# Softmax inverses from a logarithm, an exponential and one Newton step, a first pair of heads in three units, and a new order of the attention's work

## The chip, the cores and the metric

The kernel runs on one core of one Trainium2 chip. A core has five engines that run side by side, each with its own instruction stream that it works through in order: TensorE (PE, matrix products; its weight loads are listed as PEld), VectorE (DVE), ScalarE (ACT), GpSimd (POOL) and SyncE (SP, which here only issues DMA transfers). They wait for one another through semaphores. The metric is the device time of one execution in microseconds. An engine that waits for a semaphore holds up everything that stands behind it in its own stream, so the order in which work is written to the streams decides as much as the amount of it.

## The reference

```python
def _attn_ref(q, k, v):                     # 2 x 8 heads, 1152 rows, 64 wide
    q_pool = q.reshape(B, H, S // 2, 2, D).mean(axis=3)      # 576 pooled queries
    scores = scale * np.matmul(q_pool, k.transpose(0, 1, 3, 2))
    scores = scores - np.max(scores, axis=-1, keepdims=True)
    attn = np.exp(scores)
    attn = attn / (np.sum(attn, axis=-1, keepdims=True) + 1e-09)
    return np.matmul(attn, v)

def _moe_ref(x, w_in, w_out):               # 1152 x 512, 2048 hidden
    h = x @ w_in
    g = np.maximum(h, 0.0) + np.log1p(np.exp(-np.abs(h)))
    return g @ w_out

def _moe2_ref(x, w1, w2, w3, w_out):        # 768 hidden
    h = np.maximum(np.maximum(x @ w1, x @ w2), x @ w3)
    return h @ w_out
```

All of it is float32, and the weights arrive as 64-bit floats. The attention's output goes through the first dense block, and that one's through the second.

## The kernel before

**Two stages.** First the attention of 16 heads, taken as 8 pairs; then the dense blocks, which are one long chain of products on PE. The kernel computes a fast form of the attention with ordinary f32r products and checks at the end, with one flag, that its sums were in a safe range; a slower exact form stands behind a branch (`guarded`) and is not run here. Only the fast form (the `else` branch) and the flag are touched by the change.

**A pair of heads, first pass.** `add_q` adds neighbouring queries, `turn_q` and `turn_k` transpose on PE, `high_q`, `low_q`, `high_k`, `low_k` split them into a high and a low part, and `send_q`, `send_q3`, `send_k`, `send_k3` move these by DMA into the stacked operands `q1`, `q3`, `k1`, `k3`. `scores` then multiplies 9 rows of queries (128 each) with the keys in three groups of 384, each into one bank, and `part_max` on DVE reduces each bank to a maximum (tile `nh`, 27 reductions a pair). `whole_max` joins the three groups (`nm`), `turn_m` transposes the maxima on PE, `keep_m` copies them on ACT, and `send_m` puts them by DMA into the last row of `q3`, from which the second pass subtracts them inside the product. This happens in two steps: six rows, then three.

**A pair of heads, second pass: two units.** A unit is one half of a pair's queries: 288 columns for both heads. For each of 9 key blocks j, `turned` computes the transposed scores of both heads (tile `st`, two products each), `exps` exponentiates them on ACT into one of 9 buffers (`p`), `add_p` adds the block to a running sum `acc` over 2 x 288 columns (7 of a unit's 8 adds on POOL, the last on DVE), and `values` multiplies with v into the bank `x` (in two groups, after 4 and after 9 blocks). Then `sum_up` (tile `l`) sums `acc` over the partitions on PE, `keep_sum` copies it on ACT into `rr` and adds the 1e-9, `inverse` takes the reciprocal on DVE in one instruction, `divide` multiplies it with `x` into the output `xy`, and `note` adds the inverses into `low_sums` on POOL for the flag. A unit has one of two `x` banks; all other products share six single banks. After the second unit of pairs 0 to 3, `high_x` and `low_x` split the output for the dense stage.

**Weights.** Nine of the dense blocks' weight tiles are made during the attention: `load_weight` (SP), `size_weight` (ACT), `bound_weight` (POOL, tile `size`), three steps of `float_weight` (DVE, tile `t`), `high_weight` (ACT), `low_weight` (DVE, tile `wl`). Their place is behind everything else (`late`), so they go wherever the planner sees an engine free.

**What sets the order.** `Order` is a planner that runs when the kernel is built. Each piece of work is added with an engine, an assumed duration and a place (a due time); the planner starts, at each engine that comes free, the piece with the lowest place that could start then, and the result is written into the streams. The assumed durations are therefore part of the program: before the change a step of `float_weight` is taken to last 0.5 to 0.7, `low_weight` 0.69, `inverse` 0.45, an add on DVE 0.8, an add on POOL 1.4.

```python
                    engine = "DVE" if j in ON_DVE else "POOL"        # ON_DVE = (8,)
                    order.add(engine, 1.4 if engine == "POOL" else 0.8, p, add_p, u, j, engine,
            order.add("DVE", 0.45, p - 3, inverse, u, writes=(f"rr{u % 2}",))
            order.add("POOL", 0.85, p, note, u, reads=(f"rr{u % 2}",), writes=("low",))
                    order.add("DVE", (0.5, 0.7, 0.7)[step], late + 2 + step, float_weight, n, step,
```

## Time and profile before

| | us |
|---|---|
| median of three runs | 663.94 (663.5 to 664.76) |
| the profiled execution: its own time | 661.27 |
| the profiled execution: span of its trace | 659.5 |
| first product of the second pass (tile `st`) | 31.15 |
| first product of the dense stage | 293.54 |

| share of the span | PE | DVE | ACT | POOL |
|---|---|---|---|---|
| busy | 93% | 69% | 48% | 62% |

The profile is one execution, 1.77 us longer outside the trace than inside. The attention fills the first 293.5 us of it and the dense stage the other 366.0 us; the dense stage keeps PE busy 97% of the time, the attention does not. The busy shares are averages over both, so the attention is read stretch by stretch: which engine has no idle time left in a stretch, and how long a unit takes there. The granted clock (PEclk) is the share of full speed that PE was allowed; PE has two levels, 2.4 and 1.2 GHz.

### The profile page before, as it was taken

The numbers are of one execution on the slowest core, as the hardware profiler recorded it, in microseconds if no ns is written. First come the engines' busy times: TensorE is split into PE (matmuls) and PEld (weight loads), VectorE is DVE, ScalarE is ACT, GpSimd is POOL, SyncE is SP. The second block draws the span as 40 slices with busy tenths as digits, with TensorE's granted clock in tenths as the row PEclk, the third lists the DMA queues.
The fourth block names the chain that finished last, engine by engine and source line by source line (L and its number), as shares of the span: only waits on it lengthen the run. The fifth ranks groups of instructions, "written<-read, shape, count | busy, mean of one in ns | idle before, by whom it ended". The sixth has DMA issues, their size and how long they took to land.

```text
span 659.5 us, 10134 instructions
## 1 busy us (share of the span) xinstructions
PE 610.3 (93%) x3548; PEld 531.5 (81%) x3548; DVE 455.6 (69%) x769; ACT 319.7 (48%) x769; POOL 406.4 (62%) x338
## 2 busy tenths in 40 slices
PE   4899999689886999977999999999999999999995
PEld 3677777457564677656999999999999999999995
DVE  4957777997899887449888888898888852222221
ACT  3245556345453565546677767776664321111111
POOL 6179898867886698877988878789794500000000
PEclk9899999799788999998999999999999999999998
DMA  7997697557626470002333433332233400000001
GB/s 175 199 201 186 125 236 177 150 136 171 157 59 169 104 185 10 1 1 65 99 95 111 127 100 114 95 125 94 67 90 104 126 1 30 20 0 18 32 1 53
DMA packets 60621, 66.14 MB, mean 100 GB/s; under 512 B 22224, under 2 KB 48912, under 8 KB 60560
## 3 DMA queue, kind: packets, MB, share of 16 engines
q1 hardware_dynamic: 59712, 64.62, 37.3%
q10 hardware_dynamic: 848, 0.77, 0.5%
q8 instruction: 30, 0.49, 0.3%
q14 instruction: 31, 0.25, 0.1%
HBM read 43.52 MB, written 2.36 MB: 70 GB/s over the span
## 4 chain that ended last, share of the span: by engine, by line
PE 78%; DVE 12%; POOL 4%; issue 2%; DMA 1%; ACT 1%; SPq 0%; POOLq 0%; ACTq 0%; DVEq 0%
PE bank_h_m L1260 17%; PE bank_h L1260 15%; PE bank_y L1260 15%; PE x L1033 8%; PE bank_o L1260 6%; PE st L1008 5%; PE s L958 4%; PE st L1009 4%; DVE nh L964 3%; DVE rr L1054 2%; POOL acc L1025 2%; DVE t L255 1%; PE tk L914 1%; DVE t L246 1%; POOL size L235 1%
## 5 line engine op out<-in xcount | busy, mean ns | idle before, releaser
L1025 POOL TENSOR_TENSOR acc<-acc,p 128x576 f32<-128x576 f32 x96 | 139.3, 1451 | 19.2 <-ACT p L1018 13.4
L1018 ACT ACTIVATE p<-st 128x288 f32<-128x288 f32 x288 | 101.2, 411 | 75.0 <-PE st L1009 67.7
L964 DVE TENSOR_REDUCE nh<-s 128x1 f32<-128x384 f32 x216 | 106.7, 548 | 33.6 <-PE s L958 30.6
L1260 PE MATMUL bank_h_m<-x,wh 128*128 128x384 f32 x432 | 113.2, 336 | 0.0
L1260 PE MATMUL bank_h<-x,wh 128*128 128x384 f32 x384 | 106.4, 340 | 0.4 <-DVE gl L1337 0.4
L235 POOL TENSOR_SCALAR size<-size 128x512 f32<-128x512 f32 x56 | 85.4, 1528 | 17.2 <-ACT size L230 17.0
L1008 PE MATMUL st<-q,k 128*128 128x288 f32 x288 | 88.3, 321 | 5.4 <-DVE nh L964 5.3
L1009 PE MATMUL st<-q,k 65*128 65x288 f32 x288 | 82.6, 301 | 0.0
L1033 PE MATMUL x<-p,v 128*64 128x288 f32 x576 | 81.5, 430 | 0.0
L1260 PEld LDWEIGHTS bank_h_m<-x,wh 128*128 128x128 f32 x432 | 78.3, 188 | 0.7
L1260 PE MATMUL bank_h_m<-x,wl 128*128 128x384 f32 x216 | 72.5, 335 | 0.0
L1260 PEld LDWEIGHTS bank_h<-x,wh 128*128 128x128 f32 x384 | 71.1, 191 | 1.2 <-DVE gl L1337 0.7
L1008 PEld LDWEIGHTS st<-q,k 128*128 128x128 f32 x288 | 56.0, 195 | 18.9 <-DVE nh L964 7.8
L958 PE MATMUL s<-k,q 128*128 128x384 f32 x192 | 63.3, 385 | 6.9 <-ACT p L1018 3.9
L1260 PE MATMUL bank_y<-gh,wh 128*128 128x384 f32 x192 | 65.4, 341 | 4.0 <-ACT gh L1332 2.3
L1313 POOL TENSOR_TENSOR d<-e,d 128x384 f32<-128x384 f32 x48 | 49.1, 1023 | 27.5 <-DVE d L1306 25.4
L1033 PEld LDWEIGHTS x<-p,v 128*64 128x64 f32 x576 | 40.5, 144 | 31.5 <-issue 10.8
L1260 PE MATMUL bank_h<-x,wl 128*128 128x384 f32 x192 | 65.3, 340 | 0.0
L1260 PE MATMUL bank_y<-gl,wh 128*128 128x384 f32 x192 | 65.2, 340 | 0.0
L1260 PE MATMUL bank_y<-gh,wl 128*128 128x384 f32 x192 | 65.0, 339 | 0.0
L1009 PEld LDWEIGHTS st<-q,k 65*128 65x128 f32 x288 | 56.0, 194 | 0.0
L958 PEld LDWEIGHTS s<-k,q 128*128 128x128 f32 x192 | 35.2, 201 | 20.6 <-DVE nh L964 7.0
(228 smaller groups left out, 1126.7 us busy)
## 6 DMA issues: line engine op xcount, KB each, us to landing
raw<-in_moe_w_out_dram SPq DMA_DIRECT2D x22, 512.0 KB
raw<-in_moe_w_dram SPq DMA_DIRECT2D x18, 512.0 KB
raw<-in_moe_w_in_dram SPq DMA_DIRECT2D x16, 512.0 KB
k<-kh SPq DMA_DIRECT2D x28, 288.0 KB
k<-in_k_dram SPq DMA_DIRECT2D x16, 288.0 KB
v<-in_v_dram SPq DMA_DIRECT2D x16, 288.0 KB
k<-kl SPq DMA_DIRECT2D x15, 288.0 KB
q<-qh SPq DMA_DIRECT2D x29, 144.0 KB
```

The lines of the kernel that those rows point to most:

```text
L235: nc.gpsimd.tensor_scalar(out=size, in0=size, scalar1=SMALLEST, scalar2=None, op0=ALU.max)
L246: nc.vector.tensor_scalar(out=t, in0=size, scalar1=3, scalar2=REST, op0=ALU.logical_shift_left, op1=ALU.bitwise_and,)
L958: nc.tensor.matmul(to, q1[:, i, c0 : c0 + QB], k1[:, i, cols], start=True, stop=True)
L964: nc.vector.tensor_reduce(out=tiles["nh", pr][:, at, g : g + 1], in_=tiles[n][:, :BK], axis=AX.X, op=ALU.max, negate=True)
L1008: nc.tensor.matmul(to, k1[:, i, cols], q_of(pr, i, b * HQ, (b + 1) * HQ), start=True, stop=False)
L1009: nc.tensor.matmul(to, k3[:, i, cols], q3[:, i, b * HQ : (b + 1) * HQ], start=False, stop=True)
L1018: nc.scalar.activation(out=tiles["p", u, j][:, some[0]], in_=tiles[n][:, :HQ], func=AF.Exp)
L1025: engine.tensor_tensor(out=acc, in0=tiles["p", u, 0] if j == 1 else acc, in1=tiles["p", u, j], op=ALU.add)
L1033: nc.tensor.matmul(x[halves(i)], tiles["v", u // 2][:, i, j], tiles["p", u, j][:, i], start=(j == 0), stop=(j == NJ - 1),)
L1054: nc.vector.reciprocal(tiles["rr", u], tiles["rr", u])
L1260: nc.tensor.matmul(ps, lhs(a, kk), rhs(bb, kk), start=start and n == 0, stop=stop and n == last)
L1313: nc.gpsimd.tensor_tensor(out=d, in0=gs["e", i], in1=d, op=ALU.subtract)
```

## The change

**Inverse.** The reciprocal on DVE goes. ACT takes the logarithm of the sum (`log_sum`) and the exponential of its negative (`near_inverse`), and DVE improves that by one Newton step in two instructions (`inverse`, steps 0 and 1); `divide` takes the sign back. The flag's second sum now comes out of the exponential, and `note` and `low_sums` go.

**Adds.** POOL makes all 8 adds of every unit but the last; in the last unit DVE makes all 8.

**Units.** The first pair's queries are cut in three units (128, 224, 224 columns), which makes 17 units in all. Its maxima are taken in another order of rows and in three steps, and its shift rows are written by products with the identity whose single output row ACT copies into `q3` (`row_m`, `keep_row`), without a DMA. `values` works in three groups of three blocks.

**Order.** The assumed durations are set to others, and all places (`AK`, `WINDOW`) change.

```diff
-ON_DVE = (8,)
-VALUES = ((0, 1, 2, 3), (4, 5, 6, 7, 8))
+ON_DVE = ((), ())
+VALUES = ((0, 1, 2), (3, 4, 5), (6, 7, 8))
+XB = 2
+LAST = (1, 2, 3, 4, 5, 6, 7, 8)
...
+        UNIT = [(0, 0, P), (0, P, (NQ - P) // 2), (0, (NQ + P) // 2, (NQ - P) // 2)]
+        UNIT += [(pr, b * HQ, HQ) for pr in range(1, NPAIR) for b in range(2)]
+        FIRST_ROWS = (0, 5, 4, 1, 6, 2, 7, 3, 8)
+        FIRST_STEPS = ((0, 3), (3, 7), (7, 9))
...
+        def row_m(step, n):
+            a, z = rows_of(0, step)
+            tm = bank(n, f"tm_0_{step}")
+            for k, x in enumerate(sorted(FIRST_ROWS[a:z])):
+                at = FIRST_ROWS.index(x)
+                nc.tensor.matmul(tm[D : D + 1, k * P : (k + 1) * P], maxima(0)[:, at : at + 1], ident, start=True, stop=True)
+
+        def keep_row(step, part, n):
+            a, z = rows_of(0, step)
+            k, r, count = runs(sorted(FIRST_ROWS[a:z]))[part]
+            nc.scalar.copy(shift_row(0)[:, r * P : (r + count) * P], tiles[n][D : D + 1, k * P : (k + count) * P])
...
-        def inverse(u):
-            nc.vector.reciprocal(tiles["rr", u], tiles["rr", u])
-        def note(u):
...
+        def log_sum(u):
+            tiles["rz", u] = sm.tile([P, HQ], F32, tag="rz", name=f"rz_{u}")
+            W = UNIT[u][2]
+            nc.scalar.activation(out=tiles["rz", u][:, :W], in_=tiles["rr", u][:, :W], func=AF.Ln)
+
+        def near_inverse(u):
+            rz = tiles["rz", u][:, : UNIT[u][2]]
+            nc.scalar.activation(out=rz, in_=rz, func=AF.Exp, scale=-1.0, accum_out=sums[:, 1, u : u + 1])
+
+        def inverse(u, step):
+            W = UNIT[u][2]
+            rr, rz = tiles["rr", u][:, :W], tiles["rz", u][:, :W]
+            if step == 0:
+                nc.vector.tensor_tensor(out=rr, in0=rr, in1=rz, op=ALU.mult)
             else:
+                nc.vector.scalar_tensor_tensor(out=rr, in0=rr, scalar=2.0, in1=rz, op0=ALU.subtract, op1=ALU.mult)
...
-                    engine = "DVE" if j in ON_DVE else "POOL"
-                    order.add(engine, 1.4 if engine == "POOL" else 0.8, p, add_p, u, j, engine,
+                    engine = "DVE" if j in (ON_DVE[u % 2] if u + 1 < UNITS else LAST) else "POOL"
+                    order.add(engine, 1.5 * part if engine == "POOL" else 1.25 * part, p, add_p, u, j, engine,
...
-                    order.add("DVE", (0.5, 0.7, 0.7)[step], late + 2 + step, float_weight, n, step,
+                    order.add("DVE", (1.2, 1.25, 1.25)[step], late + 2 + step, float_weight, n, step,
```

The dense stage's code and its order on every engine are the same before and after. Three places in the streams show what moved. In the names the first number is the unit (in `nh`, `nm` and `s` the pair), the second the key block or query row, and the last one is only the tile's running number.

POOL, one unit in the stretch where weights are made. Before, unit 6 (from its first add to the next `low_sums`):

```order
L1025 TENSOR_TENSOR acc_6_1601<-p_6_0_1555,p_6_1_1589 128x576
L235 TENSOR_SCALAR size_2_1612<-size_2_1612 128x512
L1025 TENSOR_TENSOR acc_6_1601<-acc_6_1601,p_6_2_1596 128x576
L1025 TENSOR_TENSOR acc_6_1601<-acc_6_1601,p_6_3_1631 128x576
L1025 TENSOR_TENSOR acc_6_1601<-acc_6_1601,p_6_4_1656 128x576
L812 TENSOR_TENSOR qs_6_1705<-q_6_1342 128x2x4x64
L817 TENSOR_TENSOR qt_6_1707<-qm_6_1343 64x128
L1025 TENSOR_TENSOR acc_6_1601<-acc_6_1601,p_6_5_1695 128x576
L1025 TENSOR_TENSOR acc_6_1601<-acc_6_1601,p_6_6_1718 128x576
L1025 TENSOR_TENSOR acc_6_1601<-acc_6_1601,p_6_7_1732 128x576
L1060 TENSOR_TENSOR low_sums_121<-low_sums_121,rr_5_1792 128x288
```

and after, unit 6 again:

```order
L1061 TENSOR_TENSOR acc_6_1534<-p_6_0_1482,p_6_1_1496 128x576
L1061 TENSOR_TENSOR acc_6_1534<-acc_6_1534,p_6_2_1526 128x576
L1061 TENSOR_TENSOR acc_6_1534<-acc_6_1534,p_6_3_1552 128x576
L1061 TENSOR_TENSOR acc_6_1534<-acc_6_1534,p_6_4_1564 128x576
L237 TENSOR_SCALAR size_0_1468<-size_0_1468 128x512
L1061 TENSOR_TENSOR acc_6_1534<-acc_6_1534,p_6_5_1617 128x576
L237 TENSOR_SCALAR size_1_1498<-size_1_1498 128x512
L1061 TENSOR_TENSOR acc_6_1534<-acc_6_1534,p_6_6_1652 128x576
L1061 TENSOR_TENSOR acc_6_1534<-acc_6_1534,p_6_7_1672 128x576
L1061 TENSOR_TENSOR acc_6_1534<-acc_6_1534,p_6_8_1684 128x576
```

POOL now makes the eighth add and no `low_sums`; the sizes of the first weights, which stood in units 5 and 6, come a unit later (in all, one or two a unit until unit 15).

DVE, the end of a unit where weights begin. Before, around the inverse of unit 4:

```order
L974 TENSOR_REDUCE nm_3_1_1550<-nh_3_1193 128x3
L246 TENSOR_SCALAR t_0_1553<-size_0_1380 128x512
L255 SCALAR_TENSOR_TENSOR t_0_1553<-raw_0_1252,t_0_1553 128x512
L259 SCALAR_TENSOR_TENSOR t_0_1553<-raw_0_1252,t_0_1553 128x512
L1054 RECIPROCAL rr_4_1566<-rr_4_1566 128x288
L1066 TENSOR_TENSOR xy_99<-x_4_1240,rr_4_1566 128x288
L246 TENSOR_SCALAR t_1_1594<-size_1_1474 128x512
L1025 TENSOR_TENSOR acc_5_1390<-acc_5_1390,p_5_8_1538 128x576
L255 SCALAR_TENSOR_TENSOR t_1_1594<-raw_1_1383,t_1_1594 128x512
```

and after, around the inverse of unit 5:

```order
L977 TENSOR_REDUCE nh_3_1346<-s_3_7_2_1632 128x1
L1103 TENSOR_TENSOR rr_5_1634<-rr_5_1634,rz_5_1646 128x288
L1105 SCALAR_TENSOR_TENSOR rr_5_1634<-rr_5_1634,rz_5_1646 128x288
L1117 SCALAR_TENSOR_TENSOR xy_99<-x_5_1348,rr_5_1634 128x288
L977 TENSOR_REDUCE nh_3_1346<-s_3_8_0_1667 128x1
L977 TENSOR_REDUCE nh_3_1346<-s_3_8_1_1670 128x1
L977 TENSOR_REDUCE nh_3_1346<-s_3_8_2_1674 128x1
L994 TENSOR_REDUCE nm_3_1567<-nh_3_1346 128x3
L248 TENSOR_SCALAR t_0_1711<-size_0_1468 128x512
```

The inverse now stands in front of the last reductions and no weight stands in front of it; the nine weights are spread over units 6 to 15, about one a unit, where they stood in units 4 to 10.

PE, where the second pass begins. Before:

```order
L958 MATMUL s_0_8_2_323<-k1_0_181,q1_0_102 128x384
L914 MATMUL tk_1_0_328<-ident_94,k_1_284 128x128 x3
L914 MATMUL tk_1_1_333<-ident_94,k_1_284 128x128 x3
L914 MATMUL tk_1_2_344<-ident_94,k_1_284 128x128 x3
L841 MATMUL tq_2_0_350<-ident_94,qs_2_272 128x128 x3
L841 MATMUL tq_2_1_356<-ident_94,qs_2_272 128x128
L845 MATMUL tq_2_1_356<-ident_94,qt_2_274 128x64
L980 MATMUL tm_0_1_365<-ident_94,nm_0_1_362 3x128
L1008 MATMUL st_0_0_0_371<-q1_0_102,k1_0_181 128x288
```

and after:

```order
L966 MATMUL s_0_3_2_337<-k1_0_154,q1_0_102 128x384
L1030 MATMUL tm_0_0_345<-ident_94,nm_0_275 1x128 x3
L966 MATMUL s_0_8_0_350<-k1_0_154,q1_0_102 128x384
L966 MATMUL s_0_8_1_354<-k1_0_154,q1_0_102 128x384
L966 MATMUL s_0_8_2_358<-k1_0_154,q1_0_102 128x384
L1044 MATMUL st_0_0_0_360<-q1_0_102,k1_0_154 128x128
L1045 MATMUL st_0_0_0_360<-q3_0_111,k3_0_112 128x128
```

The first product of the second pass no longer stands behind the last maxima of the pair and pair 2's query transposes; it needs the maxima of three rows and their copy, and the last two rows' maxima are taken while it runs.

## Rows read from the trace of the kernel before

**Rows 1.** Busy time by stage: start:end, length, PE, PEld, DVE, ACT, POOL, PEclk, DMA share, GB/s
```profile
31.10:93.80 62.70, 62.41 (x422) 47.21 (x423) 45.40 (x85) 35.58 (x106) 50.19 (x39) 1.00 0.80 181
93.80:231.20 137.40, 114.89 (x696) 83.20 (x698) 119.78 (x175) 66.72 (x183) 105.90 (x75) 0.89 0.58 144
231.20:271.70 40.50, 40.50 (x282) 30.51 (x281) 29.97 (x52) 24.19 (x72) 34.24 (x25) 1.00 0.31 80
...
293.50:659.50 366.00, 354.72 (x1966) 345.28 (x1964) 231.01 (x406) 174.83 (x363) 184.60 (x162) 0.99 0.23 71
```

**Rows 2.** Chain of waits in time: start, length; first values of units 0, 4, 11, 14, 15
```profile
35.58 2.09 PE x L1033 x16
...
93.78 2.09 PE x L1033 x16
...
231.21 2.09 PE x L1033 x16
...
271.74 2.09 PE x L1033 x16
...
282.44 2.09 PE x L1033 x16
```

**Rows 3.** Groups of POOL instructions, 98 to 210 us: xcount, busy us, mean ns, idle before
```profile
L1025 POOL TENSOR_TENSOR acc<-acc,p 128x576 f32<-128x576 f32 x35 | 52.7, 1506 | 5.0 <-ACT p L1018 3.3
L235 POOL TENSOR_SCALAR size<-size 128x512 f32<-128x512 f32 x8 | 13.3, 1660 | 0.0
L1025 POOL TENSOR_TENSOR acc<-p,p 128x576 f32<-128x576 f32 x6 | 10.6, 1767 | 0.0
L1060 POOL TENSOR_TENSOR low_sums<-low_sums,rr 128x288 f32<-128x288 f32 x6 | 4.8, 800 | 17.0 <-DVE rr L1054 17.0
L288 POOL TENSOR_TENSOR x<-xy,x 128x384 fp32r<-128x384 f32 x3 | 3.9, 1292 | 0.0
...
L817 POOL TENSOR_TENSOR qt<-qm 64x128 f32<-64x128 f32 x3 | 2.0, 660 | 0.0
```

**Rows 4.** Groups of POOL instructions, 30 to 98 us
```profile
L1025 POOL TENSOR_TENSOR acc<-acc,p 128x576 f32<-128x576 f32 x27 | 38.2, 1414 | 3.1 <-ACT p L1018 1.3
L1025 POOL TENSOR_TENSOR acc<-p,p 128x576 f32<-128x576 f32 x5 | 8.2, 1636 | 17.1 <-ACT p L1018 17.1
L812 POOL TENSOR_TENSOR qs<-q 128x512 f32<-128x512 f32 x3 | 3.9, 1286 | 0.0
```

**Rows 5.** Groups of DVE instructions, 98 to 210 us
```profile
L1054 DVE RECIPROCAL rr<-rr 128x288 f32<-128x288 f32 x6 | 11.6, 1940 | 0.0
...
L259 DVE SCALAR_TENSOR_TENSOR t<-raw,t 128x512 int32<-128x512 int32 x7 | 9.8, 1407 | 0.1
L279 DVE TENSOR_TENSOR wl<-t,wh 128x512 fp32r<-128x512 f32 x7 | 8.3, 1185 | 0.0
L1025 DVE TENSOR_TENSOR acc<-acc,p 128x576 f32<-128x576 f32 x6 | 7.9, 1324 | 0.6 <-POOL acc L1025 0.6
```

**Rows 6.** Groups of ACT instructions, 98 to 210 us
```profile
L1018 ACT ACTIVATE p<-st 128x288 f32<-128x288 f32 x103 | 36.6, 404 | 23.8 <-PE st L1009 21.5 <-ACT p L1018 1.8
```

**Rows 7.** Timeline of the start: start us, length, engine, line, instruction, count
```profile
19.12 5.65 DVE L964 TENSOR_REDUCE nh<-s 128x1 f32<-128x384 f32 x12
...
29.19 0.16 DVE L974 TENSOR_REDUCE nm<-nh 128x3 f32<-128x9 f32 x1
29.39 1.76 DVE L928 TENSOR_TENSOR kl<-tk,kh 128x384 fp32r<-128x384 f32 x3
...
31.15 0.52 PE L1008 MATMUL st<-q,k 128*128 128x288 f32 x1
```

**Rows 8.** Timeline of PE where the dense stage begins, with the idle time before
```profile
292.90 0.71 PE L1044 MATMUL l<-acc,ones 128*64 128x288 f32 x4 [4.05 <-DVE acc L1025]
...
295.34 0.52 PE L1260 MATMUL bank_h<-x,wl 128*128 128x384 f32 x1
...
296.30 0.52 PE L1260 MATMUL bank_h<-x,wl 128*128 128x384 f32 x1
```

More of the change, by code (lines that the diff above doesn't have):

```diff
@@ L1079, in judge @@
             else:
[L1080 removed]
+                nc.vector.tensor_reduce(out=good, in_=sums, axis=AX.XY, op=ALU.add)
         counts = {"s": 0, "t": 0}
@@ L1168, in first_pass @@
-                        k += 1
+                        order.add("DVE", 0.56, p, part_max, pr, x, h, n, reads=(name_of(n),), writes=(f"nh{y}_{x}{h}",), free=n)
                 p = at + gap * k
+                some = rows(pr)[a:z]
                 n = next_bank("tm")
-                order.add("DVE", 0.2, p, whole_max, pr, step, reads=[f"nh{y}_{x}{h}" for x in ROWS[a:z] for h in range(NB)], writes=(f"nm{step}",))
-                order.add("PE", 0.12, p, turn_m, pr, step, n, reads=(f"nm{step}",), writes=(name_of(n),), take=n)
@@ new lines, in first_pass @@
+                groups = runs(sorted(some))
+                for part in range(len(groups)):
+                    order.add("ACT", 0.32, p - 3, keep_row, step, part, n, reads=(name_of(n),),
+                              writes=(f"q3{y}_{step}{part}",), free=n if part == len(groups) - 1 else None)
+        def one_unit(u):
+            pr, c0, W = UNIT[u]
+            y, part = pr % 2, W / HQ
+            b = [w for w in range(UNITS) if UNIT[w][0] == pr].index(u)
+            at, gap = WINDOW * pr + c0 / NQ * WINDOW, WINDOW / 2 / NJ * part
+            shifts = [f"q3{y}_{s}" for s in range(b + 1)]
+            if pr == 0:
+                shifts = [f"q3{y}_{s}{g}" for s in range(b + 1) for g in range(2)]
@@ L1200, in one_unit @@
-            order.add("DVE", 0.45, p - 3, inverse, u, writes=(f"rr{u % 2}",))
-            order.add("DVE", 0.47, p - 3, divide, u, reads=(f"rr{u % 2}", f"x{u % 2}"), writes=(f"xy{u}",))
-            order.add("POOL", 0.85, p, note, u, reads=(f"rr{u % 2}",), writes=("low",))
-            if b and pr < NC:
-                order.add("ACT", 0.46, p + 5, high_x, 0, pr, reads=(f"xy{u - 1}", f"xy{u}"), writes=(f"xh{pr}",))
-                order.add("POOL", 1.1, p + 5, low_x, 0, pr, reads=(f"xh{pr}",))
+                p = at + gap * js[-1] + AK["values"] * part
@@ new lines, in one_unit @@
+                order.add("PE", 0.51 * len(js) * part + 0.2, p, values, u, js,
+                          reads=[f"p{(u * NJ + j) % NPT}" for j in js] + [f"v{y}"], writes=(f"x{u % XB}",))
+            if XB == 1:
+                order.add("ACT", 0.43, p, keep_values, u, reads=("x0",), writes=(f"xc{u % 2}",))
+            n, p = next_bank("sum"), at + gap * NJ + AK["sum"] * part
+            order.add("PE", 0.7 * part, p, sum_up, u, n, reads=(f"acc{u % 2}",), writes=(name_of(n),), take=n)
+            order.add("ACT", 0.65, p - 3, keep_sum, u, n, reads=(name_of(n),), writes=(f"rr{u % 2}",), free=n)
@@ L1207 @@
+            if (u + 1 == UNITS or UNIT[u + 1][0] != pr) and pr < NC:
+                mine = [f"xy{w}" for w in range(UNITS) if UNIT[w][0] == pr]
+                order.add("ACT", 0.52, p + 5, high_x, 0, pr, reads=mine, writes=(f"xh{pr}",))
+                order.add("POOL", 1.22, p + 5, low_x, 0, pr, reads=(f"xh{pr}",))
         for pr in range(NPAIR):
```

267 lines of the change are left out of this document (148 added, 119 removed).

## The prediction

> **What bounds the kernel now.** I read the stages first, then the time a unit takes in each, then the instruction groups of the two fullest engines. From 31.1 to 93.8 us PE is busy 62.4 of 62.7 us at full clock [rows 1]: PE is the bound. Units 0 to 4 start their first values at 35.58 and 93.78 [rows 2], so a unit takes 58.2 / 4 = 14.55 us there. From 93.8 to 231.2 us no engine is full: PE 115, DVE 120, POOL 106 of 137.4 us, and PE's granted clock averages 0.89 [rows 1]. Units 4 to 11 lie in it (93.78 to 231.21, [rows 2]): 137.43 / 7 = 19.63 us each, so 7 x 5.08 = 35.6 us are lost against the PE-bound rate. The one thing that is in this stretch and in no other is the making of weights: 1.2 to 1.4 us for a step on DVE [rows 5] where the planner counted 0.5 to 0.7, and 1.94 us for an inverse where it counted 0.45. DVE is 87% busy and the rest is engines waiting in a wrong order. After that units 11 to 14 take 13.5 us (40.5 / 3, [rows 1]) and unit 14 takes 10.7 (271.74 to 282.44, [rows 2]), having less and less first-pass work beside them. The dense stage fills 366 us with PE at 97% [rows 1]; it is written in the same order before and after, so the change is worth what it moves the dense stage's start, 293.5 us.
>
> **The change, part by part.**
>
> *DVE* loses per unit the reciprocal (1.94) and the add (1.32, [rows 5]), and gets two short instructions over 288 columns. None like them is in the trace: the nearest row is the add over twice the columns, 1.32 in this stretch [rows 5], so at most 1.3 each and at least a quarter of that; I take half, 0.66. Net 3.26 - 1.32 = 1.94 us less per unit, and the weights' 5 us come one a unit (units 6 to 15) instead of nine in seven units. Before, DVE did 119.8 us in 3.5 pairs = 34.2 a pair [rows 1]; less 2 x 1.94, and less 0.57 of a weight at some 5 us (nine in 3.5 pairs were 2.57 a pair, now 2), is about 27.4 a pair, under PE's 29.1 (2 x 14.55). DVE stops being the bound.
>
> *ACT* gets a logarithm and an exponential a unit; the nearest row is the exponential of one block, 0.40 [rows 6], so 1 us a unit with the accumulator's read. ACT is busy 67 of 137 us there [rows 1]; DVE's shorter inverse pays that latency back, and the bank it frees is wanted only a unit later. I count nothing; if ACT were full it would cost 1 us x 17.
>
> *POOL* gets the eighth add (1.51, [rows 3]) for the sum it loses (0.80): 0.7 us more a unit. The sum for POOL in the stretch with weights: a unit is 7 x 1.506 + 1.767 = 12.31 us of adds; a pair has besides qs 1.29 [rows 4], qt 0.66, and, for the first four, x 1.29; a weight's size is 1.66 [rows 3].
> - Units 3 and 4: 24.6 + 1.29 + 0.66 + 1.29 = 27.9.
> - Units 5 to 10, three pairs with two sizes each: 27.9 + 3.3 = 31.2, together 93.6.
> - Units 11 to 15, one size each: 5 x 13.97 = 69.9.
>
> Together 191.4 us. PE at 14.55 a unit up to unit 10, 13.5 to unit 13 and 10.7 after needs 8 x 14.55 + 3 x 13.5 + 2 x 10.7 = 178.3 for the same thirteen units. **POOL becomes the bound**, at about 31 us a pair where the old order took 39.3.
>
> *The start.* The 27 reductions of pair 0 end at 29.19 and the second pass begins at 31.15 [rows 7]. In the new order its first product needs only the maxima that stand before the last six reductions: 29.2 - 6 x 0.47 (5.65 / 12, [rows 7]) = 26.4, and 0.3 for two more joins. The three row products on PE and two copies on ACT are not in the trace; I give them 2 us, between 1 and 4. That is 28.7; the bounds are 27, and 31.2 if the three differences kl (1.76, [rows 7]), which now stand in front of the last six, push everything. The first pair is then PE's: 29.1 us, and about 2 us for a third unit with its 36 narrower score products and its values (bounds 0 and 4). POOL starts unit 3 when two of its blocks are there, which I put 1.6 us before the pair's last values are through: 28.7 + 29.1 + 2 - 1.6 = 58.2.
>
> *The end.* After POOL's last add (unit 15), PE sums it up (0.71, [rows 8]), does unit 16's nine blocks of values, 2.09 x 9 / 4 = 4.7 [rows 2], its last three blocks of scores (1.6), and the last sum (0.7); unit 15's inverse stands between the fourth and fifth of DVE's adds of unit 16, which I give 0.7. That is 8.4 us.
>
> *Sum.* 58.2 + 191.4 + 8.4 = 258.0. For waits in order I add 3% of POOL's part, 6 us: the PE-bound stretch lost under 1% of PE [rows 1], the stretch with the wrong prices 13% of DVE. The dense stage starts at 264, 29.5 us sooner. Before it, PE waited 4.05 us, and then its products came 0.32 us apart (295.34 to 296.30 for three, [rows 8]) instead of the stage's 366 / 1966 = 0.19: PE at the lower of its two levels, 1.2 GHz, about 2 us lost in the first 4. I count half of that as saved: 30.5 us in all. The profiled execution's own time is 661.27 us (span 659.5), so 630.8; the median of the runs, 663.94, is 0.4% above it, which makes 633.
>
> **A rule against this change.** In the stretch with weights POOL's adds take 1.506 and 1.767 us [rows 3], before it 1.414 and 1.636 [rows 4]: POOL pays about 0.1 us an add for what DVE does beside it. The Trainium skill, page "SBUF — State Buffer", section "Who interferes with whom", says that a DVE instruction with two SBUF inputs and a GpSimd instruction that reads SBUF exclude each other, the later one blocking fully until the first is done. By that rule the reciprocal, with one input, cost POOL nothing, and each of the two Newton instructions costs it something; but the add that leaves DVE had two inputs too. The trace agrees in direction; how much the short ones cost no row shows. What it would do here is the third rival.
>
> **The rivals.**
>
> *PE stays the bound.* If POOL keeps its early prices, a unit's adds are 7 x 1.414 + 1.636 = 11.53, 0.78 less, 10 us over thirteen units; without waits the dense stage would start at 248. PE's own work ends later: 28.7 + 11 x 14.55 + 3 x 13.5 + 2 x 10.7 + 2 = 252.7. So 40.8 us sooner, 41.8 with the clock: 619.5, as a median 622. For it: POOL ran 50.2 of 62.7 us beside a full PE [rows 1]. Against it: the weights are still made, only spread out. 17%.
>
> *The new order waits as much as the old.* If the bound engine loses 13% again, POOL's 191.4 becomes 220, 22.6 us more than I sum: 656. For it: DVE at 27.4 and PE at 29.1 a pair stand close under POOL's 31, and PE's score products share six banks with DVE's reductions. Against it: the durations the order was planned with are now near the rows'. 15%.
>
> *POOL is shut out (the slower side).* If every DVE instruction with two inputs stopped POOL for its whole length, nine weights with 2 x 1.41 + 1.19 us (two steps t and wl, [rows 5]) and thirteen inverses with 2 x 0.66 would add 36 + 17 = 53 us, of which the prices of [rows 3] already hold 13 x 0.78 = 10: 43 us more, 676. It decides from 30.5 us more on, adds of 1.8 us in the mean instead of 1.54. Against it: as many such instructions raised the adds by 0.1 only. 5%.
>
> *The change doesn't do what it says:* the start gains nothing, POOL's extra add and the waits eat the rest, and the dense stage begins within a microsecond of 293.5. 3%.
>
> **How the numbers follow.** My forecast, POOL-bound at 633 (625 to 643 with the start between 27 and 31.2 and the waits between 1% and 8%), has 60%. With the other cases at 622, 656 and 676, the range for 8 in 10 reaches from 620 to 655. A difference under 0.2% (1.3 us) can't be told from none here. Faster: 60 + 17 + 15 = 92%; same 3%; slower 5%.
>
> **What would show it.** In the profile after: POOL without idle time from about 60 us to the last add of unit 15, at 1.45 to 1.55 us an add; pairs 31 us apart; PE's waits short and put down to POOL's adds, at the sums l; PEclk near 1 through the attention; DVE under 90% everywhere; the second pass beginning at 27 to 31 us, the dense stage at 256 to 273. I am wrong if the adds take over 1.7 us, if PE waits for DVE's reductions as before, if the transfers of the next pair, now due every 31 instead of 39 us, arrive late (in the fast stretch the queues were 80% busy, [rows 1], and PE full), or if the new start is not earlier.

## The result, and the profile after

| | before | after |
|---|---|---|
| median of the runs, us | 663.72 (662.4 to 664.76) | 646.37 (643.09 to 648.59) |
| profiled execution, us | 661.27 | 643.09 |
| span, us | 659.5 | 641.3 |
| mean granted clock | 0.966 | 0.985 |

The ratio is 0.9742, with a 95% interval from 0.9712 to 0.9772: 17 us less in the medians, 18.2 in the profiled executions. The forecast was 30.5 less.

The stages of the changed kernel, from its trace (columns as in [rows 1]):

```profile
0.00:30.00 30.00, 19.49 (x71) 12.45 (x71) 18.59 (x44) 9.69 (x22) 11.92 (x24) 0.83 0.79 182
30.00:65.00 35.00, 34.91 (x276) 28.25 (x278) 20.29 (x46) 21.31 (x78) 25.47 (x26) 1.00 0.72 168
65.00:111.00 46.00, 45.48 (x306) 32.75 (x303) 28.71 (x57) 27.66 (x83) 39.37 (x31) 1.00 0.77 184
111.00:207.00 96.00, 93.87 (x609) 66.55 (x608) 92.79 (x147) 61.45 (x176) 92.75 (x62) 1.00 0.69 164
207.00:250.00 43.00, 42.10 (x277) 29.76 (x274) 42.06 (x67) 26.68 (x79) 41.51 (x27) 1.00 0.39 98
250.00:272.00 22.00, 20.54 (x148) 14.00 (x147) 15.23 (x16) 14.67 (x46) 15.23 (x10) 1.00 0.08 25
272.00:641.00 369.00, 357.69 (x1964) 347.91 (x1963) 228.15 (x405) 175.66 (x366) 183.84 (x161) 0.99 0.22 70
```

The stretch that answers to the middle line of [rows 1] is 111 to 250 us. PE, DVE and POOL are all busy 97 to 98% of it and the granted clock is 1.00, where the kernel before had 84%, 87%, 77% and 0.89. The first add of a unit on POOL marks how far the kernel is. Here are units 0, 3, 6, 12 and 15 of the 17 of the changed kernel (timeline; start, length):

```profile
31.99 0.73 POOL L1061 TENSOR_TENSOR acc<-p,p 128x256 f32<-128x256 f32 x1 [7.33 <-ACT p L1052]
...
65.21 1.40 POOL L1061 TENSOR_TENSOR acc<-p,p 128x576 f32<-128x576 f32 x1
...
111.32 1.43 POOL L1061 TENSOR_TENSOR acc<-p,p 128x576 f32<-128x576 f32 x1 [1.07 <-ACT p L1052]
...
206.67 1.40 POOL L1061 TENSOR_TENSOR acc<-p,p 128x576 f32<-128x576 f32 x1
...
250.21 1.86 POOL L1061 TENSOR_TENSOR acc<-p,p 128x576 f32<-128x576 f32 x1
```

and the same places in the kernel before, which has 16 units, so that its unit 2 begins the second pair as unit 3 does above (units 2, 5, 11 and 14):

```profile
60.67 1.99 POOL L1025 TENSOR_TENSOR acc<-p,p 128x576 f32<-128x576 f32 x1
...
106.19 1.41 POOL L1025 TENSOR_TENSOR acc<-p,p 128x576 f32<-128x576 f32 x1
...
226.71 1.42 POOL L1025 TENSOR_TENSOR acc<-p,p 128x576 f32<-128x576 f32 x1
...
269.03 1.94 POOL L1025 TENSOR_TENSOR acc<-p,p 128x576 f32<-128x576 f32 x1
```

| stretch | before, us | after, us | gained, us |
|---|---|---|---|
| start to the second pair | 60.67 | 65.21 | -4.5 |
| three units | 45.52 | 46.11 | -0.6 |
| six units with weights | 120.52 (20.1 each) | 95.35 (15.9 each) | +25.2 |
| three units | 42.32 | 43.54 | -1.2 |
| the rest, to the dense start (293.54, 271.75) | 24.51 | 21.54 | +3.0 |
| dense stage, to the end of the span | 365.96 | 369.55 | -3.6 |

So nearly all of the gain lies in one stage, and the first pair and the dense stage gave 8 us of it back. Here are its six units, before and after (columns as in [rows 1]):

```profile
106.19:226.71 120.52, 99.69 (x593) 72.15 (x594) 106.71 (x153) 58.89 (x162) 92.05 (x65) 0.87 0.57 142
```

```profile
111.32:206.67 95.35, 93.22 (x604) 66.08 (x604) 92.15 (x146) 60.88 (x175) 92.42 (x61) 1.00 0.69 164
```

Of the 25.2 us, 18.7 are idle time of PE that went (20.8 against 2.1 us), and 6.5 are busy time: about as many products took 99.7 us at a mean granted clock of 0.87 and 93.2 us at 1.00. The waits that went are these: first the kernel before, 98 to 230 us (engine, line, what it waited for: us in all, times, longest), then the changed one, 90 to 280:

```profile
PE tq L841 <- DVE nh L964: 10.6, 2, 6.0
PE st L1008 <- DVE nh L964: 5.3, 5, 2.8
PE s L958 <- ACT p L1018: 3.9, 2, 2.6
PE tk L914 <- DVE nh L964: 1.6, 1, 1.6
...
```

```profile
PE s L962 <- DVE nh L977: 1.5, 4, 0.5
PE st L1044 <- DVE nh L977: 1.5, 2, 1.0
PE l L1081 <- POOL acc L1061: 1.2, 1, 1.2
PE l L1081 <- DVE acc L1061: 0.2, 1, 0.2
```

Before, PE stood 17.5 us because a bank of scores had not been reduced yet: the reductions nh were queued behind the weights' steps on DVE.

### The profile page after: what moved, and what is told of

Same layout as the page of the kernel before. It is cut to its first block, busy times and chain, and to the rows that moved or that the text cites. A ratio compares the mean times of both kernels' runs of the same rounds, so it can differ in the third digit from the quotient of the medians.

```text
span 641.3 us, 10400 instructions
## 1 busy us (share of the span) xinstructions
PE 614.1 (96%) x3640; PEld 531.7 (83%) x3640; DVE 445.8 (70%) x779; ACT 337.1 (53%) x844; POOL 410.1 (64%) x338
## 4 chain that ended last, share of the span: by engine, by line
PE 77%; DVE 14%; POOL 3%; ACT 2%; DMA 2%; issue 1%; SPq 1%; POOLq 0%; ACTq 0%; DVEq 0%
PE bank_h_m L1341 18%; PE bank_y L1341 15%; PE bank_h L1341 14%; PE x L1069 7%; PE bank_o L1341 6%; PE st L1044 5%; DVE nh L977 5%; PE s L966 4%; PE st L1045 3%; DVE rr L1105 2%; POOL acc L1061 2%; DVE t L248 2%; DVE t L261 1%; DVE t L257 1%; DMA k<-in_k_dram 1%
## 5 line engine op out<-in xcount | busy, mean ns | idle before, releaser
L1061 POOL TENSOR_TENSOR acc<-acc,p 128x576 f32<-128x576 f32 (+2 forms) x112 | 158.8, 1417 | 16.7 <-ACT p L1052 9.0
L1052 ACT ACTIVATE p<-st 128x288 f32<-128x288 f32 (+2 forms) x306 | 102.3, 399 | 67.5 <-PE st L1045 64.9
L237 POOL TENSOR_SCALAR size<-size 128x512 f32<-128x512 f32 x56 | 87.3, 1559 | 17.3 <-ACT size L232 17.1
L1044 PE MATMUL st<-q,k 128*128 128x288 f32 (+2 forms) x306 | 90.7, 317 | 1.7 <-DVE nh L977 1.5
L1045 PE MATMUL st<-q,k 65*128 65x288 f32 (+2 forms) x306 | 83.4, 292 | 0.0
L1069 PE MATMUL x<-p,v 128*64 128x288 f32 (+2 forms) x612 | 80.8, 400 | 0.0
L1044 PEld LDWEIGHTS st<-q,k 128*128 128x128 f32 x306 | 57.9, 189 | 23.8 <-issue 11.0
L1069 PEld LDWEIGHTS x<-p,v 128*64 128x64 f32 x612 | 39.2, 136 | 26.8 <-issue 7.7
L1045 PEld LDWEIGHTS st<-q,k 65*128 65x128 f32 x306 | 58.2, 190 | 0.0
L966 PE MATMUL s<-k,q 128*128 128x384 f32 x192 | 53.9, 381 | 2.5 <-DVE q L880 1.4
L1456 DVE TENSOR_TENSOR mg<-bank_h_m,mg 128x384 f32<-128x384 f32 x18 | 10.0, 555 | 61.3 <-PE bank_h_m L1341 61.3
```

What stands on the lines that cost most here:

```text
L237: nc.gpsimd.tensor_scalar(out=size, in0=size, scalar1=SMALLEST, scalar2=None, op0=ALU.max)
L966: nc.tensor.matmul(o, q1[:, i, c0 : c0 + QB], k1[:, i, cols], start=True, stop=True)
L1044: nc.tensor.matmul(to, k1[:, i, cols], q_of(pr, i, c0, c0 + W), start=True, stop=False)
L1045: nc.tensor.matmul(to, k3[:, i, cols], q3[:, i, c0 : c0 + W], start=False, stop=True)
L1052: nc.scalar.activation(out=tiles["p", u, j][:, some[0], :W], in_=tiles[n][:, :W], func=AF.Exp)
L1061: engine.tensor_tensor(out=acc, in0=first, in1=tiles["p", u, j][:, :, :W], op=ALU.add)
```

## The experiments

Ratios are to the kernel before, run beside each; the changed kernel's is 0.9742. "Us a unit" is the mean over the six units with weights, from first adds as above.

| kernel | median us | ratio, 95% interval | us a unit | dense start |
|---|---|---|---|---|
| changed kernel | 646.4 | 0.974 (0.971 to 0.977) | 15.9 | 271.8 |
| e_recip | 642.5 | 0.968 (0.965 to 0.972) | 15.7 | 270.9 |
| e_psum | 645.4 | 0.973 (0.969 to 0.976) | 15.6 | 273.9 |
| e_eighth | 643.8 | 0.973 (0.970 to 0.977) | 15.5 | 272.2 |
| e_recip_eighth | 643.1 | 0.971 (0.967 to 0.974) | 15.5 | 270.8 |
| e_half_no | 635.6 | 0.958 (0.956 to 0.960) | 15.1 | 264.6 |
| e_two16 | 641.2 | 0.968 (0.964 to 0.971) | 15.9 | 270.5 |
| e_places | 643.4 | 0.970 (0.968 to 0.972) | 16.4 | 273.8 |
| e_order | 643.9 | 0.972 (0.968 to 0.976) | 15.7 | 275.1 |
| e_prices | 639.0 | 0.965 (0.961 to 0.968) | 14.9 | 266.0 |
| e_weights | 656.5 | 0.990 (0.988 to 0.993) | 17.6 | 288.3 |
| e_last | 636.2 | 0.959 (0.957 to 0.961) | 14.9 | 262.7 |

### The new inverse taken back (e_recip)

```diff
-            nc.scalar.activation(out=tiles["rz", u][:, :W], in_=tiles["rr", u][:, :W], func=AF.Ln)
+            pass
...
-            nc.scalar.activation(out=rz, in_=rz, func=AF.Exp, scale=-1.0, accum_out=sums[:, 1, u : u + 1])
+            pass
...
-                nc.vector.tensor_tensor(out=rr, in0=rr, in1=rz, op=ALU.mult)
-            else:
-                nc.vector.scalar_tensor_tensor(out=rr, in0=rr, scalar=2.0, in1=rz, op0=ALU.subtract, op1=ALU.mult)
+                nc.vector.reciprocal(rr, rr)
...
```

> The changed kernel at its own order and places, but the inverse is one reciprocal on VectorE again (no Ln and Exp on ScalarE, no Newton step); VectorE's second operation of the inverse is gone and the first is the reciprocal. Theory A (VectorE is still the bound of units 5 to 13, because its operations with two operands in SBUF are stretched while GpSimd adds: the two steps of the new inverse take 0.73 + 1.36 = 2.08 us there, the reciprocal took 1.94): within 2 us of the changed kernel, 643 to 648 us. Theory B (as forecast: GpSimd's adds are the bound and VectorE has room): also within 2 us, by hiding, but VectorE's busy share in units 5 to 13 rises above its 98%, which it cannot, so a loss of 0 to 5 us. Theory C (the new inverse is worth what the forecast wrote, 1.94 - 1.32 = 0.62 us a unit on a full VectorE): 5 to 8 us slower, 651 to 654.

Measured: 642.5 us, not slower and perhaps 4 us faster (the profiled executions are level, 643.04 and 643.09), so theory C is out. On a DVE that is 98% full, Ln, Exp and two Newton operations are worth no more than the one reciprocal of 1.94 us in [rows 5]. The mean of the two Newton operations in the units with weights, 120 to 240 us, is 0.73 + 1.36 = 2.08 us.

### Why two short operations take 2 us (e_psum)

```diff
-                nc.vector.tensor_tensor(out=rr, in0=rr, in1=rz, op=ALU.mult)
+                nc.vector.tensor_tensor(out=l, in0=l, in1=rz, op=ALU.mult)
...
-                nc.vector.scalar_tensor_tensor(out=rr, in0=rr, scalar=2.0, in1=rz, op0=ALU.subtract, op1=ALU.mult)
+                nc.vector.scalar_tensor_tensor(out=rr, in0=l, scalar=2.0, in1=rz, op0=ALU.subtract, op1=ALU.mult)
```

Here l is the PSUM bank of the sums, kept until the second operation. The planner counts 0.46 us for each of the two instead of 0.6, so the order is another too.

> The changed kernel with one edit: the Newton step takes the row sums from their PSUM bank (and leaves the first product there), so that neither of its two VectorE operations has two operands in SBUF; the bank is held until the second one. Theory A (VectorE is the bound of units 5 to 13 and is stretched by GpSimd's adds): both steps take 0.46 us like the division, whose one operand is in PSUM, and does so in every unit; that is 2.08 - 0.92 = 1.16 us less a unit, 8 to 11 units that are full: 6 to 12 us faster, 634 to 640. Theory B (GpSimd's adds are the bound): the steps shrink all the same, the time stays within 2 us, 644 to 648. A loss of 2 to 5 us would say that the bank held some 3 us longer is missed by the score products.

The view by source line gives shortest, median and longest in ns, 90 to 270 us. The changed kernel: a reduction and a division (one operand in PSUM) and the two Newton operations (both in SBUF):

```profile
L977 DVE TENSOR_REDUCE nh<-s x138: 540/546/559, 91.5 to 247.5; 128x1 f32<-128x384 f32 x138
...
L1103 DVE TENSOR_TENSOR rr<-rr,rz x12: 441/508/1580, 102.3 to 266.3; 128x288 f32<-128x288 f32 x12
...
L1105 DVE SCALAR_TENSOR_TENSOR rr<-rr,rz x13: 458/1557/1565, 90.0 to 266.8; 128x288 f32<-128x288 f32 x13
...
L1117 DVE SCALAR_TENSOR_TENSOR xy<-x,rr x13: 457/457/459, 90.5 to 267.4; 128x288 f32<-128x288 f32 x13
```

and the two in e_psum:

```profile
L1104 DVE TENSOR_TENSOR l<-l,rz x13: 448/456/466, 89.8 to 269.4; 128x288 f32<-128x288 f32 x13
...
L1106 DVE SCALAR_TENSOR_TENSOR rr<-l,rz x13: 457/457/458, 90.3 to 269.9; 128x288 f32<-128x288 f32 x13
```

With both operands in SBUF the second operation takes 0.46 us or about 1.56, hardly anything between: it stands for 1.1 us, less than one of POOL's adds lasts (shortest 1.40). With one in PSUM it is 0.457 every time. The Trainium skill, "SBUF — State Buffer", "Who interferes with whom", says that a DVE instruction with two SBUF inputs and a GpSimd instruction that reads SBUF exclude each other. The trace agrees, and says who pays most here: DVE, by 1.1 us. POOL pays too, but about 0.1 us an add (1.52 in the mean of units 3 to 15, 1.40 at the shortest).

So the mechanism of theory A is shown, but not its consequence: 1.2 us less DVE work a unit gave 0.3 us a unit, 1.9 us over units 6 to 11. Then, in unit 12, the order spoils it. DVE's next weight step waits for POOL's size, and the reductions, and with them PE, wait behind it (timeline of DVE, then of PE, in e_psum):

```profile
204.25 1.62 DVE L248 TENSOR_SCALAR t<-size 128x512 int32<-128x512 int32 x1 [2.78 <-POOL size L237]
205.79 2.87 DVE L977 TENSOR_REDUCE nh<-s 128x1 f32<-128x384 f32 x6
```

```profile
206.39 0.69 PE L966 MATMUL s<-k,q 128*128 128x384 f32 x1 [3.02 <-DVE nh L977]
```

Unit 12 takes 19.5 us instead of 13.9. What the edit is worth in an order without that wait stays open; up to there it is a quarter of what DVE saves.

### The eighth add given back to DVE (e_eighth, e_recip_eighth)

```diff
-ON_DVE = ((), ())
+ON_DVE = ((8,), (8,))
```

> The changed kernel with the eighth add of every unit but the last on VectorE again, as in the kernel before; the order is planned again with that. GpSimd has 1.51 us less a unit, VectorE 0.75 to 1.9 us more. Theory A (VectorE is the bound of units 5 to 13): 8 to 14 us slower, 654 to 660. Theory B (GpSimd is the bound from unit 3 on): 5 to 12 us faster, until TensorE's 14.5 us a unit. Theory C (TensorE is the bound throughout, the other two only fill up): within 3 us.

Measured: 643.8 us, theory C. Both savings undone at once:

> The changed kernel with both of its savings on VectorE undone: reciprocal in place of Ln, Exp and Newton step, and the eighth add of all units but the last on VectorE. Alone they gave 642.5 and 643.8 us beside 646.4 of the changed kernel. Theory T (TensorE's own work is what bounds units 3 to 13 now, at some 15.5 us a unit; VectorE and GpSimd only fill the time): 641 to 647 us. Theory V (VectorE is at the edge, either load fits and both don't: 1.3 us a unit over 8 units too much): 650 to 658 us.

Measured: 643.1, theory T. Inside a unit, the two savings on DVE together are worth nothing that these runs can tell.

### Work left out on both (e_half_no)

```diff
-        nc.gpsimd.tensor_scalar(out=size, in0=size, scalar1=SMALLEST, scalar2=None, op0=ALU.max)
+        pass
...
-                out=tiles["nh", pr][:, at, g : g + 1], in_=tiles[n][:, :BK], axis=AX.X, op=ALU.max, negate=True
+                out=tiles["nh", pr][:, at, g : g + 1], in_=tiles[n][:, : BK // 2], axis=AX.X, op=ALU.max, negate=True
```

> The changed kernel with less work on both full engines: VectorE takes the maximum of a third's first 192 keys instead of all 384, and GpSimd's bound of the weights' sizes is left out; so the shift is not the row's maximum, and a size is not bounded. It takes some 0.2 x 13.5 = 2.7 us a unit from VectorE's operations on PSUM and 1.77 us from GpSimd. Theory T (TensorE's own work bounds units 3 to 13; the two only fill its time): 0 to 4 us faster than the changed kernel, 642 to 646, with VectorE below 85% and GpSimd below 90% in the full stage. Theory V (VectorE and GpSimd together bound the full stage, 8 units at 16.0 us): 8 units by 1.3 us, down to TensorE's 14.7: 9 to 12 us faster, 634 to 637.

Measured: 635.6 us, the time of theory V. Where it came from speaks for neither alone. From 120 to 240 us, first e_recip, then e_eighth, then e_half_no (columns as above):

```profile
120.00:240.00 120.00, 119.35 (x781) 85.25 (x777) 118.34 (x180) 71.73 (x202) 116.30 (x77) 1.00 0.65 157
```

```profile
120.00:240.00 120.00, 116.19 (x757) 82.39 (x754) 112.43 (x183) 72.89 (x213) 98.57 (x66) 1.00 0.62 148
```

```profile
120.00:240.00 120.00, 119.10 (x782) 85.51 (x780) 101.71 (x185) 78.10 (x226) 105.30 (x72) 1.00 0.63 153
```

With DVE at 85% and POOL at 88%, PE is full at 15.1 us a unit. That is about PE's own pace in this order; the changed kernel's 15.9 is 0.8 above it, and this 0.8 is what the work left out on DVE and POOL was worth there (4.5 us over six units). The second pair begins 2.2 us earlier as well (63.05). The dense start moves by 7.1 us; the medians differ by 10.8, mostly because the profiled execution of the changed kernel lies 3.3 us under its median. e_eighth fits this: POOL falls to 82%, and a unit changes by 0.4 us only, with PE at 97% and DVE at 94%.

### The durations alone (e_prices, e_weights, e_order)

e_prices is the kernel before with the change's durations. The main ones:

```diff
-                    order.add(engine, 1.4 if engine == "POOL" else 0.8, p, add_p, u, j, engine,
+                    order.add(engine, 1.5 if engine == "POOL" else 1.25, p, add_p, u, j, engine,
...
-            order.add("DVE", 0.45, p - 3, inverse, u, writes=(f"rr{u % 2}",))
+            order.add("DVE", 1.95, p - 3, inverse, u, writes=(f"rr{u % 2}",))
...
-                    order.add("DVE", (0.5, 0.7, 0.7)[step], late + 2 + step, float_weight, n, step,
+                    order.add("DVE", (1.2, 1.25, 1.25)[step], late + 2 + step, float_weight, n, step,
...
-                order.add("DVE", 0.69, late + 7, low_weight, n, reads=(f"t{n % 2}", f"w{n}"), writes=(f"wl{n}",))
+                order.add("DVE", 1.05, late + 7, low_weight, n, reads=(f"t{n % 2}", f"w{n}"), writes=(f"wl{n}",))
```

> The kernel before with the change's durations in the planner and nothing else: its own places, WINDOW 27.76, its own functions. Theory O1 (the durations alone let the order account for VectorE's real load): 645 to 655 us. Theory O2 (durations and places belong together; the old places were found with the old durations): 657 to 672 us, no gain.

Measured: 639.0 us, less than either theory expected, and faster than the whole change (0.961 to 0.968 against 0.971 to 0.977). PE's waits of 98 to 230 us are one line, and the stage is full of PE:

```profile
PE st L1008 <- DVE nh L964: 0.3, 1, 0.3
```

```profile
120.00:240.00 120.00, 119.44 (x811) 88.09 (x809) 114.80 (x182) 72.55 (x206) 111.42 (x79) 1.00 0.58 139
```

811 products where the changed kernel has 760, in 120 us, at 14.9 us a unit, with the reciprocal and the eighth add still on DVE. So the order by itself is enough for the gain, and the durations by themselves are enough for that order.

> The kernel before with four durations changed in the planner and nothing else: those of a weight piece (VectorE's three steps 1.2, 1.25 and 1.25 us instead of 0.5, 0.7 and 0.7, its low part 1.05 instead of 0.69, ScalarE's 0.68 and 0.61 instead of 0.57 and 0.52). All durations together gave 639.0 us. Theory W (the weights, 2.59 us in the planner and 5.15 in the trace, are what made VectorE late for the maxima of units 4 to 11): 638 to 645 us. Theory I (it is the inverse, 0.45 us in the planner and 1.94 in the trace, and the eighth add, 0.8 and 1.32, that come once in every unit): 652 to 664.

Measured: 656.5, theory I: the weights' durations alone bring 6.7 of some 23 us, and PE still waits 5.9 us for nh before the products st from 98 to 230 us. The rest, some 16 us, comes with the other durations: the inverse and the add, wrong by 1.5 and 0.45 us in every unit, must matter, or one of the smaller durations that e_prices also corrects; these were not taken apart.

> The kernel before with all its functions (reciprocal on VectorE, the eighth add on VectorE, the note on GpSimd, two units in the first pair, shift rows by DMA), but ordered with the change's durations and places (WINDOW, AK, the values in three groups of three). Theory O (nearly all of the change's gain is the order: TensorE no longer waits in units 4 to 11, and the functions only move work between VectorE and GpSimd): 643 to 650 us. Theory F (the functions carry it, as the forecast's sum of removed VectorE work has it: 2.6 us less a unit over 8 full units): 655 to 668 us.

Measured: 643.9, theory O. But the change's places, with the values in threes, are 5 us worse for the old functions than the old places are, the opposite of O2 above. The total hides one thing, since the dense stage is 4 us shorter in e_order than in the changed kernel (see the last part). Next to e_two16 below, which has the change's functions at the same places and also two units in the first pair, e_order is level up to unit 14 (its first add, e_order, then e_two16) and then waits for the last unit's sum (PE's waits of e_order, 248 to 276 us):

```profile
248.27 1.60 POOL L1025 TENSOR_TENSOR acc<-p,p 128x576 f32<-128x576 f32 x1 [2.90 <-ACT p L1018]
```

```profile
248.16 1.87 POOL L1061 TENSOR_TENSOR acc<-p,p 128x576 f32<-128x576 f32 x1
```

```profile
PE l L1044 <- DVE acc L1025: 5.2, 1, 5.2
...
```

From there to the dense start e_order takes 26.8 us and e_two16 22.3, where this wait is 0.2. So at these places the functions bring nothing inside the units; what they bring, 4.6 us, lies at the end, where DVE makes the last unit's adds.

### The first pair (e_two16)

```diff
-        UNIT = [(0, 0, P), (0, P, (NQ - P) // 2), (0, (NQ + P) // 2, (NQ - P) // 2)]
+        UNIT = [(0, 0, HQ), (0, HQ, HQ)]
...
-        FIRST_ROWS = (0, 5, 4, 1, 6, 2, 7, 3, 8)
-        FIRST_STEPS = ((0, 3), (3, 7), (7, 9))
+        FIRST_ROWS = ROWS
+        FIRST_STEPS = STEPS
```

> The changed kernel with the first pair as before: two units of 288 columns instead of three of 128, 224 and 224, and its shift rows sent by DMA instead of made by products. The forecast took the start with three units as 28.7 us to the first transposed product plus 29.1 + 2 - 1.6 to the first add of unit 3 (58.2); the changed kernel shows 30.9 and 65.2. Theory A (the three narrow units cost TensorE, which has no gap there, more than the earlier start gives): 2 to 5 us faster, first add of the second pair at 61 to 63 us. Theory B (the start is lost to the order that waits for k's transfer, whatever the units): within 1.5 us. Theory C (the three units gain as the forecast has it): 2 to 4 us slower.

This first form still counted 17 units in its guard, so the exact path ran behind it (1275.5 us); its time says nothing of the edit. The second form:

> The changed kernel with the first pair as before (two units of 288 columns, shift rows sent by DMA), the guard's count set for 16 units; this stands for e_two, whose guard still counted 17 units and which therefore also ran the exact path and has no use as a time of this edit. Theory A (the three narrow units cost TensorE, which has no gap there, more than the earlier start gives): 2 to 5 us faster than the changed kernel, the first add of the second pair at 61 to 63 us instead of 65.2. Theory B (the start is lost to the order that waits for k's transfer, whatever the units): within 1.5 us. Theory C (the three units gain as the forecast has it): 2 to 4 us slower.

Measured: 641.2 us, 5 us less than the changed kernel; the intervals (0.964 to 0.971 and 0.971 to 0.977) touch, and the profiled executions are 1.8 us apart (641.31 and 643.09). Theory A in the medians, but not by its mechanism: the second pair begins at 64.60, only 0.6 us earlier. The first adds of units 0 and 2:

```profile
37.42 1.44 POOL L1061 TENSOR_TENSOR acc<-p,p 128x576 f32<-128x576 f32 x1 [19.21 <-ACT p L1052]
...
64.60 1.41 POOL L1061 TENSOR_TENSOR acc<-p,p 128x576 f32<-128x576 f32 x1
```

Its first product st is at 35.11 us, in the changed kernel at 30.29 (not 30.9, as written above): the three units do start the second pass 4.8 us sooner. Then they need 34.9 us to the second pair, two units 29.5. Two things take the head start back. Scores that e_two16 does before the second pass now stand inside it: PE does 30 score products ahead of its first st against 43 in e_two16, and from there to the first add of the second pair 31 (7.3 us of PE) against 18 (4.4). And a narrow product st is not a cheap one. From the chain of the changed kernel, 128 columns (unit 0), then 288 (two stretches):

```profile
31.37 0.11 PE st L1044
...
34.08 0.81 PE x L1069 x12
```

```profile
139.34 0.13 PE st L1045
139.47 1.61 PE x L1069 x12
```

The values x of 128 columns take half as long as those of 288 (0.068 and 0.134 each), the products st 0.11 against 0.13. At 0.11 to 0.115 the first pair's 108 st products cost some 12.2 us, 72 wide ones 9.7.

Against the kernel before only the second holds. It too does 30 score products ahead of its first st, and 30 from there to its second pair, which begins at 60.67, 29.5 us after that st. What differs is the products st in this stretch, those of the next pair that fall into it included (tile st alone, before, then after: stretch, length, PE, PEld, ACT, PEclk, DMA share, GB/s):

```profile
31.15:60.67 29.52, 14.41 (x82) 12.02 (x82) 13.95 (x41) 0.99 0.81 177
```

```profile
30.29:65.21 34.92, 18.25 (x120) 15.51 (x120) 16.54 (x60) 1.00 0.72 168
```

They make 3.8 of the 5.4 us by which the changed kernel's first pair is longer.

### The places (e_places)

```diff
-WINDOW = 31.77
+WINDOW = 27.76
...
-VALUES = ((0, 1, 2), (3, 4, 5), (6, 7, 8))
+VALUES = ((0, 1, 2, 3), (4, 5, 6, 7, 8))
```

with the old AK and two units in the first pair.

> All functions of the changed kernel (Ln, Exp and Newton step, no eighth add on VectorE, no note, the last unit's adds on VectorE) and its durations, but two units in the first pair and the places of the kernel before (WINDOW 27.76, its AK, the values in groups of four and five). With the change's places this was 641.2 us; the old functions at the new places were 643.9 and at the old places 639.0. Theory P (the new places are worse than the old once the durations are right, by some 5 us, whatever the functions): 634 to 638 us. Theory N (the new places belong to the new functions): 642 to 650.

Measured: 643.4 us, theory N in time. The new functions at the old places take 16.4 us a unit, and PE waits 5.3 us for nh before the products s, from 98 to 230 us; the old functions take 14.9 there. The old functions do better at the old places, by 5 us; the new ones at neither (641.2 and 643.4, with intervals that overlap). So the places can't be judged without the functions.

### A faster kernel (e_last)

```diff
-                    engine = "DVE" if j in ON_DVE else "POOL"
+                    engine = "DVE" if u + 1 == UNITS or j in ON_DVE else "POOL"
```

in e_prices.

> The kernel before with the change's durations and one part of the change more: all eight adds of the last unit on VectorE, as in the changed kernel. With the durations alone TensorE waits 4.5 us for the last unit's last add before its sums, and the dense products begin after a stretch at a granted clock of 0.91; the changed kernel waits 0.2 us there. Theory L (the wait goes, nothing else is late there): 3 to 5 us faster than with the durations alone, 634 to 636. Theory D (ScalarE's last exponentials are late next): 0 to 2 us faster, 637 to 639.

Measured: 636.2 us, ratio 0.959 (0.957 to 0.961), faster than before and than the changed kernel, and at the near edge of theory L (the dense start comes 3.3 us sooner than in e_prices). PE's idle times around the dense start, first e_prices, then e_last:

```profile
264.83 1.23 PE L1044 MATMUL l<-acc,ones 128*64 128x288 f32 x4 [4.49 <-DVE acc L1025]
284.63 0.69 PE L1260 MATMUL bank_y<-gh,wh 128*128 128x384 f32 x1 [5.82 <-ACT gh L1332]
```

```profile
262.06 0.71 PE L1044 MATMUL l<-acc,ones 128*64 128x288 f32 x4 [2.31 <-DVE acc L1025]
281.17 0.69 PE L1260 MATMUL bank_y<-gh,wh 128*128 128x384 f32 x1 [6.23 <-ACT gh L1332]
```

Half of the wait for the last sum is gone. The next one, 6.2 us for the first gh, is untouched, and the granted clock from 281 to 291 us is 0.53: there is more to be had at the start of the dense stage.

## Why the prediction was right in sign and put the gain too high

The median of 646.4 us lies in the range for 8 in 10, 620 to 655, but outside the 625 to 643 of my own forecast, between it and the second rival. It isn't there for that rival's reason: in the stretch with weights PE waits about 2 us where it waited 20. The two terms that missed most, the start and the dense stage, are in no rival at this price.

- **What bounded the kernel.** That engines wait in a wrong order for which wrong durations are to blame stood in the first part. e_prices shows it: the durations alone give more than the whole change.
- **DVE stops being the bound.** Wrong. I put DVE at 27.4 us a pair; from 111 to 207 us, three pairs, it is 92.79 / 3 = 30.9, or 97%. The term that was mis-sized most is the Newton operation: 0.66, measured 1.04 in the mean, up to 1.36 for the second, which makes 1.5 of the 3.5 us. The bounds, 0.33 and 1.3, held the mean; the row I scaled was stretched by POOL already (1.32 in the mean, 0.75 at its shortest), and the stretch doesn't shrink with the columns. A weight's four steps on DVE took 5.4 us where I counted 5, which is 0.9 more; the rest I can't place. But by e_recip the price of the inverse hardly moves the time.
- **ACT at nothing.** Right as far as the runs show: Ln, Exp and the accumulator's read take 0.45 + 0.44 + 0.19 = 1.08 us a unit, for which I had put 1, and ACT is busy 61 of 96 us; e_recip, without them and with the reciprocal back, gains at most 4 us.
- **POOL becomes the bound.** The sum was right: units 3 to 15 take 198.6 us from the first add (65.21) to the end of the last (263.8), forecast 191.4 + 6. The adds take 1.52 us in the mean, forecast 1.54. Pairs are 29 to 33 us apart. But the word "bound" was too strong, and that the sum came out is in part luck: e_eighth takes an add a unit from POOL and gains 0.4 us of 1.5, and from 65 to 111 us PE is busy 99% of the time and POOL 86%. There a unit takes 15.4 us, nearly the 15.9 of the stretch where all three are full.
- **PE's price.** I took 14.55 us a unit from the old order, the rival "PE stays the bound" too. In the new order e_half_no shows 15.1 with PE at 99%. Why the same products cost more there was not taken apart; e_prices, with values in two groups a unit instead of three, has 14.9.
- **The start.** 58.2 forecast, 65.21 measured: 7 of the 12.3 us that are missing. The first st came at 30.29, not 28.7, inside its bounds. The term that failed is the first pair's length, 29.1 + 2 - 1.6 = 29.5; it took 34.9. Two parts of it were too small. For two units it counts 27.5 us, where the trace of the kernel before has 29.5 (31.15 to 60.67). And the third unit cost 5.4 us instead of 2, above the bound of 4: it makes 36 more products st, and the narrower ones are hardly cheaper, as the part on e_two16 shows.
- **The end and the waits.** 8.4 forecast, 7.95 measured (263.8 to 271.75); beyond the sum of 191.4 there were 7 us, forecast 6. POOL's idle time was more, 11.9 of 198.6 us: the durations that I added up overlap a little from one instruction to the next, so that 191.4 us of them fill only 186.7. More than half of it lies before 111 us, so the sign "POOL without idle time from about 60 us" did not come true.
- **The dense stage.** Forecast 1 us shorter, measured 3.6 longer. The restart went as forecast: in its first 38 us PE does 181 products against 173, 1.4 us ahead. Then each product is slower, about which the next part speaks.
- **The rule against this change** and its rival. The two engines do exclude each other, but it is mostly DVE that stands; POOL's adds stayed at 1.52, about as forecast, and the slow case was 33 us off.

In sum: 7.0 at the start, 1.2 in POOL's part, -0.5 at the end and 4.6 in the dense stage make the 12.3 us between 630.8 and 643.09.

## What to carry to other kernels

Where a planner sets the order, put measured durations into it first and time that alone: here that gave 23 us, where the whole change gave 17. An engine that shows 98% busy beside two others at 97 and 98% is not yet the bound; take work away from it and see whether the time moves. Work that is cut into narrower pieces must be priced by the number of the pieces: three units instead of two made 36 more products st, and a narrow one cost 0.11 us where a wide one cost 0.13.
